# Attention of two batches in step, its second tiles in the weights' empty half, and x of the last two batches through device memory

## The chip, the cores and the metric

The kernel runs on one core of one Trainium2 chip. The time is device microseconds of one execution, given as the median of several runs. TensorE (PE) multiplies, with weight loads shown apart as PEld; VectorE (DVE), ScalarE (ACT) and GpSimd (POOL) work on tiles; SyncE (SP) issues most of the DMA transfers.

## The reference

Everything is float32 except the two weight matrices, which arrive as float64. Shapes: four batches, eight heads, 768 positions, head size 64; the heads side by side give rows of 512.

```python
# decaying attention, block of 64 positions, lam per head
intra = (qb @ kb.T * Dmask) @ vb              # Dmask[i,j] = lam**(i-j) for i >= j
inter = (qb * lam**(pos+1)) @ kv_state
out[block] = intra + inter
kv_state = lam**64 * kv_state + (kb * lam**(63-pos)).T @ vb
...
x = out, heads side by side                    # (4, 768, 512)
u = x + real(fft(fft(x, axis=1), axis=2))
un = (u - mean(u)) / sqrt(var(u) + 1e-6)       # per row of 512
return u + max(un @ w_ch1, 0) @ w_ch2          # 512 x 2048, 2048 x 512
```

## The kernel before

**Attention** goes in chunks of 128 positions (two reference blocks in one), six a batch. `attn(b)` is a generator that writes the instructions of one batch, chunk by chunk. `attn_in` loads k, q and v (256 KB each), multiplies k by its decays on POOL, turns K and Q on TensorE (L314, L319) and copies them back through ScalarE (L316, L321); VectorE makes the decayed queries qs. `attn_out` makes the scores (L338), which VectorE multiplies by the decays into sc (L343), updates the state (L358 on TensorE, then POOL and VectorE), and adds the product of queries and state (L373) to that of scores and v (L379). The result oT is turned back into rows of x (L395). Batch 0 is kept turned as well (`TURNED`), and batch 1 follows it without a break, its first loads under batch 0's last chunk (`LEADS`). These two use states of 64 rows. Batches 2 and 3 use a "padded" state of 128 rows, sd, that ScalarE fills. Their attention is woven chunk by chunk into the products of the MLP.

**The transform and the layer norm** are `fft_ln(b)`. Rows and mirrored rows are folded on VectorE (L476 to L571); the mirrored ones are gathered by POOL's DMA from a copy of x in device memory. Then come products with tables of cosines and sines (L603), the transform over the width (L615 to L620), sums and the normalised rows un (L634 to L691), and transposes of these to ut (L660).

**The weights** arrive as float64 and are decoded in 32 pieces of 512 KB (`load_weights`): a load into a tile raw, Sign and Relu on ScalarE (L225, L228), and five steps on VectorE (L226, L230, L232, L234, L235). The tile raw comes from the same pool of four buffers as hr, the MLP's hidden rows. The tile e is scratch of the decoding. Both matrices stay in SBUF for the whole kernel. The first half of w1's columns and of w2's rows is decoded first, then the second half.

**The MLP** runs plainly for four groups of half a batch each (`PLAIN`): first product L749 into a PSUM bank pm, ReLU into hr on ScalarE (L757) or VectorE (L755), second product L763. The first three of these are done in two halves of the hidden width, so that the first halves can go ahead of the second half of the weights. The other four groups wait and go through a scheme that saves products by sums of blocks: `combine_weights` (L837) and `front_sums` make sums of the weights (w1s and others), and L1031, L1198 and L1124 are its products. This late stage begins at 409.57 us. Its rows are ur, its sums of rows sx.

**What sets the order.** All these generators are woven into one text by `beside` and `weave`, which draw from two generators in proportion to estimated times. A scheduler then sets each engine's row; a few instructions are held in the order written (`keep_in_program_order`). Each engine works through its row in order. PSUM is shared by two pools of banks: pa (`psum_a`) for attention and transform, pm (`psum_m`) for the MLP.

```python
run(beside(att0, NC * t_chunk - 2.7, w, 0.25 * NW))
...
fr = chain([att1, fft_ln(1)] + [front(b) for b in range(2, B)])
...
back = chain(half[1] + [mlp(*PLAIN[3])])
run(weave(fr, back, (t_back - t_half) / (t_rest - t_rest * t_half / t_back)))
```

Of the kernel before, what the change touches and what calls it, by code (L numbers as in the profile page):

```python
# [77 lines left out]
def kernel(  # L78
# [207 lines left out]
    def attn(b):  # L286

        head = () if b - 1 in LEADS else attn_in(b, 0)
        for c in range(NC):
            yield from head  # L290
            head = attn_in(b, c + 1) if c < NC - 1 else attn_in(b + 1, 0) if b in LEADS else ()
            yield from attn_out(b, c, head)

    ins, oTs, eo = {}, {}, {}
    LEADS = (0,)
# [3 lines left out]
    def attn_in(b, c):  # L299
        rows = slice(c * C, (c + 1) * C)  # L300
        kt, qt, vt = (new(ld, [C, H, D], nm) for nm in ("k", "q", "v"))
        for t, src in ((kt, k), (qt, q), (vt, v)):
            nc.sync.dma_start(t, src[b, :, rows, :].rearrange("h p d -> p h d"))
        if b == 0:
            load_tables(c)

        kd = None
        if c < NC - 1:
            kd = new(at, [C, H, D], "kd")
            nc.gpsimd.tensor_tensor(kd, kt, kpow, op=ALU.mult)  # L310

        ptk = psum_a([128, HP, C])
        for hp in range(HP):
            nc.tensor.transpose(ptk[:, hp, :], pair(kt, hp), ident)  # L314
        kT = new(at, [128, HP, C], "kT")
        nc.scalar.copy(kT, ptk)  # L316
        ptq = psum_a([128, HP, C])
        for hp in range(HP):
            nc.tensor.transpose(ptq[:, hp, :], pair(qt, hp), ident)  # L319
        qT = new(at, [128, HP, C], "qT")  # L320
        nc.scalar.copy(qT, ptq)  # L321
        qs = None
        if c > 0:
            qs = new(at, [128, HP, C], "qs")
            nc.vector.tensor_tensor(qs, ptq, qpow, op=ALU.mult)
        ins[b, c] = kT, qT, qs, kd, vt
        yield 1.2

    def attn_out(b, c, head):
        kT, qT, qs, kd, vt = ins.pop((b, c))  # L330
        last = c == NC - 1
        padded = b not in TURNED and b - 1 not in LEADS

        mm = nc.tensor.matmul
        pss = [psum_a([C, HP, C]) for _ in range(2)]
        for hp in range(HP):
            for hi in range(2):
                mm(pss[hi][:, hp, :], lhsT=kT[HD[hi], hp, :], rhs=qT[HD[hi], hp, :], start=True, stop=True)  # L338
        sc = []
        for hi in range(2):  # L340
            t = new(at, [C, HP, C], "sc", bufs=3)
            with tc.high_priority(100) if not padded else ExitStack():
                nc.vector.tensor_tensor(t, pss[hi], decay[:, hi::2, :], op=ALU.mult)  # L343
            sc.append(t)
        if last and b - 1 in LEADS:
            mirror_a(b, pin=True)
        yield 2.4 if padded and not last else 1.5


        s_old, s_new = (st, st) if padded else (turns_of[(c + 1) % 2], turns_of[c % 2])  # L350
        if padded and c == 0:
            nc.gpsimd.memset(sd, 0.0)
        if not last:
            pu = psum_a([128, HP, D])
            for hp in range(HP):
                for hi in range(2):
                    h = 2 * hp + hi
                    mm(pu[HD[hi], hp, :], lhsT=kd[:, h, :], rhs=vt[:, h, :], start=True, stop=True)  # L358
            if c == 0:
                nc.vector.tensor_copy(s_new, pu)  # L360
            else:
                nc.gpsimd.tensor_tensor(s_new, s_old, spow.broadcast_to([128, HP, D]), op=ALU.mult)
                grown = nc.vector.tensor_tensor(s_new, s_new, pu, op=ALU.add)
            if not padded:
                yield 0.9


        po = psum_a([128, HP, C])
        if c > 0:
            for hp in range(HP):  # L370
                for hi in range(2):
                    old, qh = (sd[:, hp, hi, :], qs[:, hp, :]) if padded else (s_old[HD[hi], hp, :], qs[HD[hi], hp, :])
                    mm(po[HD[hi], hp, :], lhsT=old, rhs=qh, start=(hp == 0), stop=False, skip_group_check=True)  # L373
        if padded and not last:
            for hi in range(2):
                nc.scalar.copy(sd[HD[hi], :, hi, :], st[HD[hi]])
        for hp in range(HP):
            for hi in (1, 0) if padded else (0, 1):
                mm(po[HD[hi], hp, :], lhsT=vt[:, 2 * hp + hi, :], rhs=sc[hi][:, hp, :],  # L379
                   start=(c == 0 and hp == 0), stop=(hp == HP - 1), skip_group_check=True)  # L380
        oT = new(at, [128, HP, C], "oT")
        nc.scalar.copy(oT, po)
        if b in TURNED:

            if c == 0:
                nc.scalar.copy(first, po[:, :, 0:1])
            elif c > 1:
                nc.scalar.copy(oTs[b][:, :, 0:1], po[:, :, 0:1])
        yield 2.0
        yield from head  # L390

        def turn(oT):
            px = psum_a([C, HP, 128])
            for hp in range(HP):
                nc.tensor.transpose(px[:, hp, :], oT[:, hp, :], ident)  # L395
            return px.rearrange("p h e -> p (h e)")

        def put(px, x, n=128):
            nc.scalar.copy(x[0:n, 0:HM], px[0:n, 0:HM])
            nc.scalar.copy(x[0:n, HM:DM], px[0:n, DM - 1:HM - 1:-1])  # L400

        def back(oT, x):
            put(turn(oT), x)

        if b not in TURNED:
            x = xn_[b, c] = new(xp, [C, DM], "x") if c < HC else new(xn, [C, DM], "xn")
            back(oT, x)
            if c == 0:
                xd[b] = (dram.tile([S - 256, DM], F32, name=f"xa{b}"), dram.tile([257, DM], F32, name=f"xb{b}"))
                nc.scalar.dma_start(xd[b][1][256:257], x[0:1])  # L410
            elif not last:
# [10 lines left out]
            yield 1.7  # L422
            return

# [11 lines left out]
        px = turn(oTs[b]) if c > 1 else None  # L436
# [6 lines left out]
        if c > 1:  # L443
            mirrored(c - 1, px)
            yield 1.4
        if not last:
            x = xn_[b, c] = new(xp, [C, DM], "x") if c < HC else new(xn, [C, DM], "xn")
            back(oT, x)
            yield 1.7
        else:  # L450
            mirrored(c, turn(oTs[b]))
            for t in range(HC):
                xs[b, t] = xn_.pop((b, t))
            yield 1.4
# [4 lines left out]

    uts, utd, ud, held = {}, {}, {}, {}  # L460
# [22 lines left out]
    def mirror_a(b, pin=False):  # L483

        xa = xd[b][0]

        eo[b] = new_eo()
        for a, n in enumerate(BLK):
            i = gather(out=eo[b][a][1][0:n, 1, 0:DM], out_offset=None, in_=xa[:, :], in_offset=row_of(a, n))
            if pin:  # L490

                tc.keep_in_program_order(i)
        for t in range(2, HC):
            u = xs[b, HC + t] = new(xp, [128, DM], "x")
            i = gather(out=u[:, :], out_offset=None, in_=xa[:, :], in_offset=row_of(2 + t))
            if pin:
                tc.keep_in_program_order(i)

    def mirror_b(b):
        for t in range(2):  # L500
            u = xs[b, HC + t] = new(xp, [128, DM], "x")
            gather(out=u[:, :], out_offset=None, in_=xd[b][1][:, :], in_offset=row_of(2 + t))
# [75 lines left out]
    def fft_ln(b):  # L578
# [11 lines left out]
        else:  # L590
            yield 1.0
# [744 lines left out]
    def front(b):  # L1336
        yield from attn(b)
        yield from fft_ln(b)

# [29 lines left out]
    t_chunk = 7.3  # L1369
    t_front = NC * t_chunk + 13.0 + 7.0 + 5.7 + 3 * 2.4  # L1370
# [4 lines left out]

    att1, mix = attn(1), fft_ln(0)
    att0 = attn(0)
    run(part(att0, 2.7))
# [59 lines left out]
```

## Time and profile before

| | |
|---|---|
| time, median of 3 runs | 775.78 us (774.68 to 776.88) |
| profiled execution, span | 771.7 us, 15006 instructions; no other time is given for it |
| PE busy | 752.6 us (98%) |
| PEld busy | 646.7 us (84%) |
| DVE busy | 602.8 us (78%) |
| ACT busy | 231.1 us (30%) |
| POOL busy | 178.4 us (23%) |
| DMA | 120.22 MB, mean 156 GB/s |

The span runs from the first to the last instruction of the execution. A line of the timeline gives start in us, duration in us, engine, source line, operation, output<-inputs, shapes, and in brackets how long the engine had stood idle ahead of it and what ended that. A line of the chain gives start, duration, engine, output tile, source line and number of instructions. A line of the windows gives the window, its length, then busy time and number of instructions of PE, PEld, DVE, ACT and POOL, the granted TensorE clock, the mean share of busy DMA engines and GB/s. A group's line ends with its busy time, the mean ns of one, and the idle time ahead of it. A DMA line gives KB each and the median us from issue to landing.

### The profile page before, as it was taken

To read this page: it belongs to the slowest core of one execution; us is meant where nothing else is said; L and a number is where in the kernel's file an instruction comes from. 1 tells how busy PE (TensorE), PEld (TensorE's weight loads), DVE (VectorE), ACT (ScalarE), POOL (GpSimd) and SP (SyncE) were. 2 spreads that over 40 slices of the span, in tenths; PEclk is the share of its full clock that TensorE was granted. 3 is DMA by queue.
4 is the path that set the end of the run, shared out by engine and by line. 5 is a ranking of instruction groups with operands and counts; after the bars stand their busy time and mean duration, and the time that the engine had idled before them with its cause. 6 is when DMAs were issued, how large, how long until landed. Compare 5 with 4: busy or idle time off the path is not lost.

```text
span 771.7 us, 15006 instructions
## 1 busy us (share of the span) xinstructions
PE 752.6 (98%) x5784; PEld 646.7 (84%) x5784; DVE 602.8 (78%) x1167; ACT 231.1 (30%) x532; POOL 178.4 (23%) x202
## 2 busy tenths in 40 slices
PE   6989999999999999999999999999999999999997
PEld 5777877777685967769747899999999999999997
DVE  6999998784936575336898999788986699758984
ACT  3755443435521221322101221034301341024310
POOL 3223330021111113220105941360015001230013
PEclk9999999999999999999999999999999999999999
DMA  9979732347943149731433465876545456455442
GB/s 240 274 161 250 195 125 86 106 96 181 246 117 94 45 82 270 176 97 35 113 65 124 150 218 164 273 234 202 180 124 178 125 186 182 127 175 180 144 141 70
DMA packets 154924, 120.22 MB, mean 156 GB/s; under 512 B 114286, under 2 KB 116974, under 8 KB 154854
## 3 DMA queue, kind: packets, MB, share of 16 engines
q1 hardware_dynamic: 147792, 100.51, 46.7%
q0 software_dynamic: 4032, 12.99, 4.7%
q10 hardware_dynamic: 3030, 5.78, 2.1%
q8 instruction: 46, 0.75, 0.4%
q14 instruction: 24, 0.20, 0.1%
HBM read 88.04 MB, written 31.20 MB: 155 GB/s over the span
## 4 chain that ended last, share of the span: by engine, by line
PE 88%; DVE 7%; DMA 2%; ACT 1%; issue 1%; POOL 0%; SPq 0%; DVEq 0%; ACTq 0%
PE p L1198 22%; PE p L1124 17%; PE pm L763 13%; PE pm L749 13%; PE p L1031 6%; PE pa L603 3%; PE pa L379 3%; PE pa L338 3%; PE pa L373 2%; PE pa L314 1%; PE pa L358 1%; PE pa L395 1%; DVE sc L343 1%; PE pa L763 1%; PE pa L319 1%
## 5 line engine op out<-in xcount | busy, mean ns | idle before, releaser
L749 PE MATMUL pm<-ut,w 128*128 128x256 f32 x512 | 118.3, 381 | 0.0
L763 PE MATMUL pm<-w,hr 128*128 128x512 f32 x240 | 108.7, 596 | 0.1
L749 PEld LDWEIGHTS pm<-ut,w 128*128 128x128 f32 x512 | 94.7, 190 | 14.4 <-issue 2.7
L763 PEld LDWEIGHTS pm<-w,hr 128*128 128x128 f32 x240 | 43.8, 190 | 45.5 <-issue 43.8
L1219 POOL TENSOR_TENSOR y<-y,u 128x512 f32<-128x512 f32 x12 | 19.9, 1661 | 186.8 <-DVE y L1228 155.5
L1198 PE MATMUL p<-tx,sx 128*128 128x128 f32 x400 | 52.7, 275 | 0.0
L1198 PEld LDWEIGHTS p<-tx,sx 128*128 128x128 f32 x400 | 48.6, 192 | 0.0
L1133 DVE TENSOR_TENSOR ha<-p,ha 128x512 f32<-128x512 f32 x60 | 40.1, 686 | 8.6 <-PE p L1124 8.6
L1204 ACT COPY y<-p 128x128 f32<-128x128 f32 x48 | 12.8, 266 | 103.6 <-PE p L1198 103.1
L310 POOL TENSOR_TENSOR kd<-k,decay 128x512 f32<-128x512 f32 x20 | 21.7, 1083 | 86.5 <-PE pa L358 50.1
L343 DVE TENSOR_TENSOR sc<-pa,decay 128x512 f32<-128x512 f32 x48 | 30.9, 683 | 11.7 <-PE pa L338 11.5
L1206 DVE TENSOR_TENSOR y<-p,y 128x128 f32<-128x128 f32 x92 | 25.6, 285 | 15.6 <-PE p L1198 9.1
L1198 PE MATMUL p<-w,ha 128*128 128x128 f32 x288 | 37.4, 275 | 0.0
L1133 DVE TENSOR_TENSOR hs<-p,hs 128x512 f32<-128x512 f32 x39 | 26.2, 685 | 12.4 <-PE p L1124 12.4
L338 PEld LDWEIGHTS pa<-qT,kT 64*128 64x128 f32 x384 | 25.1, 193 | 12.2 <-ACT qT L321 6.4
L1198 PEld LDWEIGHTS p<-w,ha 128*128 128x128 f32 x288 | 34.9, 192 | 0.1
L638 POOL TENSOR_SCALAR ve<-mv 128x2 f32<-128x2 f32 x12 | 6.2, 519 | 120.0 <-DVE mv L635 120.0
L757 ACT ACTIVATE hr<-pm 128x256 f32<-128x256 f32 x44 | 16.7, 382 | 57.6 <-PE pm L749 53.7
L1124 PE MATMUL p<-sx,tx 128*128 128x128 f32 x264 | 33.9, 275 | 0.0
L338 PE MATMUL pa<-qT,kT 64*128 64x128 f32 x384 | 30.1, 292 | 2.9 <-ACT qT L321 2.9
L1124 PEld LDWEIGHTS p<-sx,tx 128*128 128x128 f32 x264 | 31.7, 192 | 0.0
L379 PE MATMUL pa<-sc,v 128*64 128x128 f32 x384 | 28.9, 282 | 1.3 <-DVE sc L343 1.0
(274 smaller groups left out, 1748.4 us busy)
## 6 DMA issues: line engine op xcount, KB each, us to landing
tx<-td SPq DMA_DIRECT2D x84, 256.0 KB, 2.9
raw<-in_moe_w_ch_dram SPq DMA_DIRECT2D x32, 512.0 KB, 4.3
tx<-sd SPq DMA_DIRECT2D x63, 256.0 KB, 2.8
k<-in_k_dram SPq DMA_DIRECT2D x24, 256.0 KB, 3.7
q<-in_q_dram SPq DMA_DIRECT2D x24, 256.0 KB, 7.0
v<-in_v_dram SPq DMA_DIRECT2D x24, 256.0 KB, 5.7
td<-tx SPq DMA_DIRECT2D x21, 256.0 KB, 2.0
ud<-x SPq DMA_DIRECT2D x16, 256.0 KB, 3.1
```

What stands on the lines that cost most here:

```text
L310: nc.gpsimd.tensor_tensor(kd, kt, kpow, op=ALU.mult)
L338: mm(pss[hi][:, hp, :], lhsT=kT[HD[hi], hp, :], rhs=qT[HD[hi], hp, :], start=True, stop=True)
L343: nc.vector.tensor_tensor(t, pss[hi], decay[:, hi::2, :], op=ALU.mult)
L379: mm(po[HD[hi], hp, :], lhsT=vt[:, 2 * hp + hi, :], rhs=sc[hi][:, hp, :], start=(c == 0 and hp == 0), stop=(hp == HP - 1), skip_group_chec ...
L603: mm = nc.tensor.matmul(ps[:, n, :], lhsT=piece(a, i, n), rhs=cs[0:rows, a, i in (2, 3), n, :], start=(a == 0), stop=(a == 1))
L749: nc.tensor.matmul(ps, lhsT=w1[:, c, 128 * fc:128 * fc + 128], rhs=ut[:, c, :], start=(c == 0), stop=(c == KO - 1))
L763: return nc.tensor.matmul(ps, lhsT=hr[(fc - f0) // 4][:, fc % 4, 128 * i:128 * i + 128], rhs=w2[:, fc, :], start=(fc == f0), stop=(fc == f ...
L1031: nc.tensor.matmul(ps, lhsT=s2.A[a][:, kt, 128 * i:128 * i + 128], rhs=U[b][:, kt, :], start=(first and kt == 0), stop=(kt == 1), skip_gro ...
L1124: nc.tensor.matmul(ps[:, 128 * i:128 * i + 128], lhsT=ab[m][0][:, 128 * i:128 * i + 128], rhs=ab[m][1], start=(start and i == 0), stop=Tru ...
L1133: V.tensor_tensor(o, p, o, op=ADD)
L1198: nc.tensor.matmul(ps[:, 0:HM // 2], lhsT=ab[m][0][i], rhs=ab[m][1][:, i, :], start=(start and i == 0), stop=(i == HF // 2 - 1), skip_grou ...
L1206: V.tensor_tensor(o, ps[:, 0:HM // 2], o, op=ADD)
```

## The change

**Attention by steps.** `attention()` takes the place of `attn(b)`. A step is one chunk of two batches, first (0, 1), then (2, 3): turnings of K of both, of Q of both, scores of both, products with the state of both, state updates of both, and so on. All batches use states of 64 rows; the padded ones are gone. The next step's loads are issued at the start of a step.

**Where the second batch's tiles lie.** Batches 1 and 3 use no tiles of the pools: theirs are `spare`, slices of the second half of w2 and of w1, before these halves are decoded. (In the rows of the orders below, w_129 is w1 and w_130 is w2: where they stand in a line of attention, they are k, q, oT or another tile of the second batch.) PSUM tiles of attention alternate between pa and pm for as long as `early` is set.

**x of batches 2 and 3.** It is stored to device memory in all its rows (a third buffer, xc, for chunk 0) and loaded again in `mirrors(b)`, which also holds all gathers and is called at the start of `fft_ln(b)`.

**The order.** All attention is written ahead of the rest: the first batches' steps beside a quarter of the weights, the next ones beside the transform of batch 0 and 0.125, and the last step beside the first 12 us of the MLP and another 0.125. Then `fft_ln(1)`, `fft_ln(2)`, `front_sums` and `fft_ln(3)` stand beside the remaining half of the weights and the MLP. The late stage is as before.

```diff
-    st = const.tile([128, HP, D], F32, name="st")
-    sd = const.tile([128, HP, 2, D], F32, name="sd")
-    turns_of = [st, sd[:, 0:HP // 2].rearrange("p h a d -> p (h a) d")]
+    turns_a = [const.tile([128, HP, D], F32, name=n) for n in ("st", "sd")]
...
+    TWOS = ((0, 1), (2, 3))
+    spare = [w2[:, FO // 2 + i, :] for i in range(FO // 2)]
+    spare += [w1[:, c, DFF // 2 + DM * i:DFF // 2 + DM * (i + 1)] for c in range(KO) for i in range(2)]
...
+    def psum_t(shape):
+        bank_of[0] += 1
+        if early[0] and bank_of[0] % 8 in (1, 4, 6):
+            return psum_m(shape)
+        return psum_a(shape)
...
+        def tile(self, shape, name, i=None):
+            if self.two:
+                t = place[name if i is None else f"{name}{i % 2}"]
+                return t.rearrange("p (h d) -> p h d", h=shape[1])
+            return new(ld if name in "kqv" else at, shape, name, **({"bufs": 2} if name == "sc" else {}))
...
-            if (b, c) == (B - 1, 1):
-                with tc.issue_after(grown.ins):
-                    run(front_sums())
-            if c == NC - 2 and b - 1 not in LEADS:
-                mirror_a(b)
-            elif last:
-                mirror_b(b)
...
+    def attention():
+        steps = [([sides[b] for b in two], c) for two in TWOS for c in range(NC)]
...
+            for s in then:
+                s.load(c_)
...
+            for s in two:
+                scores(s, c)
+            yield 2.2
+            for s in two:
+                from_state(s, c)
+            if c < NC - 1:
+                for s in two:
+                    to_state(s, c)
+            yield 2.8
+            for s in two:
+                within(s, c)
+            yield 2.0
+            for f in (turn_k, turn_q):
+                for s in then:
+                    f(s, c_)
+                yield 0.6
+            for s in two:
+                back(s, c)
+                yield 0.9
...
+    def mirrors(b):
+        xa, xb, xc = xd[b]
+        eo[b] = new_eo()
...
+        if (b, 0) not in xn_:
+            for c in range(HC + 2):
+                x = xn_[b, c] = new(xp, [C, DM], "x") if c < HC else new(xn, [C, DM], "xn")
+                nc.sync.dma_start(x, xc if c == 0 else xa[(c - 1) * C:c * C])
...
-    run(beside(att0, NC * t_chunk - 2.7, w, 0.25 * NW))
-    run(beside(part(mix, T_FOLD), T_FOLD, att1, 3.25 * t_chunk))
-    run(beside(mix, 24.0, beside(att1, 2.75 * t_chunk, w, 0.16 * NW), 0.16 * NW + 1.75 * t_chunk))
+    run(beside(part(att, NC * t_step), NC * t_step, w, 0.25 * NW))
+    run(beside(part(mix, T_FOLD), T_FOLD, att, 2.0 * t_step))
+    run(beside(mix, 24.0, beside(att, 2.0 * t_step, w, 0.125 * NW), 0.125 * NW + 2.0 * t_step))
+    early[0] = False
...
-    fr = chain([att1, fft_ln(1)] + [front(b) for b in range(2, B)])
+    fr = chain([fft_ln(1), fft_ln(2), front_sums(), fft_ln(3)])
...
-    run(beside(beside(chain(half[0]), t_half, w, 0.5 * NW), t_half + 0.5 * NW, fr, t_rest * t_half / t_back + 15.0))
+    lead = chain(half[0])
+    run(beside(part(lead, 12.0), 12.0, beside(w, 0.125 * NW, att, t_step), 0.125 * NW + t_step))
+    run(att)
+    run(beside(lead, t_half - 12.0, beside(w, 0.5 * NW, fr, t_rest * t_half / t_back), 0.5 * NW + t_rest * t_half / t_back))
```

TensorE's row within attention, before, in a chunk of batch 0: one batch's transposes, then its scores and the state.

```order
L314 MATMUL pa_310<-ident,k_301 128x128 x4
L319 MATMUL pa_317<-ident,q_302 128x128 x4
L395 MATMUL pa_332<-ident,oT_299 128x128 x4
L338 MATMUL pa_339<-qT_322,kT_315 128x128
L338 MATMUL pa_340<-qT_322,kT_315 128x128
```

And after, in a step of batches 0 and 1 (L340 turns K, L348 Q, L403 turns back, L373 is the product with the state, L380 the state's update):

```order
L340 MATMUL pa_434<-ident,k_334 128x128 x4
L340 MATMUL pm_442<-ident,w_130 128x128 x4
L348 MATMUL pa_448<-ident,q_335 128x128 x4
L348 MATMUL pm_457<-ident,w_130 128x128 x4
L403 MATMUL pa_467<-ident,oT_418 128x128 x4
L403 MATMUL pa_482<-ident,w_129 128x128 x4
...
L373 MATMUL pa_525<-qs_455,sd 64x128 x8
L373 MATMUL pm_534<-w_129,w_130 64x128 x8
L380 MATMUL pa_543<-v_336,kd_432 64x64 x8
L380 MATMUL pa_554<-w_130 64x64 x8
```

Each kind of product now stands twice in a row, once for each batch, in different banks.

ScalarE's row at the MLP's first group, before: the ReLUs (L757) alternate with the Sign and Relu steps of single weight pieces.

```order
L757 ACTIVATE hr_1383<-pm_1419 128x256
L757 ACTIVATE hr_1383<-pm_1425 128x256
L225 ACTIVATE e_1432<-raw_1431 128x512
L228 ACTIVATE e_1432<-e_1432,cvt 128x512
L757 ACTIVATE hr_1472<-pm_1467 128x256
```

And after (L223 is the Sign, L226 the Relu of the decoding, L791 the ReLU of the MLP):

```order
L223 ACTIVATE e_2305<-raw_2304 128x512
L226 ACTIVATE e_2305<-e_2305,cvt 128x512
L223 ACTIVATE e_2315<-raw_2314 128x512
L791 ACTIVATE hr_2367<-pm_2362 128x256
L791 ACTIVATE hr_2367<-pm_2378 128x256
L226 ACTIVATE e_2315<-e_2315,cvt 128x512
L223 ACTIVATE e_2325<-raw_2324 128x512
```

The fifth ReLU of the first group (onto hr_2367) now stands behind the Sign of the last piece but one; the pieces ahead of it stand without MLP steps between them. On VectorE the same pieces end so, with the layer norm's un (L689) and the MLP's sums (L827) behind them:

```order
L224 TENSOR_SCALAR e_2325<-raw_2324 128x512
...
L233 SCALAR_TENSOR_TENSOR w_130<-w_130,e_2325 128x512
L689 TENSOR_SCALAR un_2426<-x_1120,mv_2116,rs_2124 128x256 x2
L827 TENSOR_TENSOR x_466<-pm_2406,x_466 128x256
```

TensorE's row ahead of the late stage, before: the last second products of the MLP stand right ahead of the first late ones.

```order
L763 MATMUL pm_3808<-w_130,hr_3566 128x512 x4
L763 MATMUL pm_3808<-w_130,hr_3678 128x512 x4
L1031 MATMUL p_3864<-ur_3775,w_129 128x256 x2
...
L1031 MATMUL p_3864<-sx_3858,w1s 128x256 x2
```

And after (L650 to L654 are the transform over the width of batch 3, L1065 is the late stage's first product):

```order
L651 MATMUL pa_3627<-dt,ys_136 128x129
L652 MATMUL pa_3627<-dt,ys_133 128x128
L1065 MATMUL p_3751<-ur_3704,w_129 128x256 x2
...
L1065 MATMUL p_3751<-sx_3745,w1s 128x256 x2
```

The MLP's products are no longer there: they stand ahead of the transform of batch 3.

More of the change, by code (lines that the diff above doesn't have):

```diff
@@ L340, in attn_out @@
         for hi in range(2):
-            t = new(at, [C, HP, C], "sc", bufs=3)
-            with tc.high_priority(100) if not padded else ExitStack():
+            t = s.tile([C, HP, C], "sc", hi)
+            with tc.high_priority(100):
                 nc.vector.tensor_tensor(t, pss[hi], decay[:, hi::2, :], op=ALU.mult)
[L344 to L365, printed above, removed]
@@ L368, in attn_out @@
-        po = psum_a([128, HP, C])
-        if c > 0:
[L370 to L380, printed above, removed]
@@ L385, in attn_out, with within @@
+    def within(s, c):
+        n, po = s.now, s.now["po"]
+        lead(mm(po[HD[hi], hp, :], lhsT=n["vt"][:, 2 * hp + hi, :], rhs=n["sc"][hi][:, hp, :],
+                start=(c == 0 and hp == 0), stop=(hp == HP - 1), skip_group_check=True)
+             for hp in range(HP) for hi in range(2))
+        n["oT"] = s.tile([128, HP, C], "oT")
+        nc.scalar.copy(n["oT"], po)
+        if s.b in TURNED:
             if c == 0:
@@ L590, in fft_ln @@
         else:
-            yield 1.0
+            mirrors(b)
+            yield 6.0
             run(fold_a(b))
```

199 lines of the change are left out of this document (107 added, 92 removed).

## Prediction

> **What bounds the kernel now.** I read the busy line and the chain of the page first, then the windows, then TensorE's groups, then the timelines of the places that the change moves.
>
> ```profile
> PE 752.6 (98%) x5784; PEld 646.7 (84%) x5784; DVE 602.8 (78%) x1167; ACT 231.1 (30%) x532; POOL 178.4 (23%) x202
> PE 88%; DVE 7%; DMA 2%; ACT 1%; issue 1%; POOL 0%; SPq 0%; DVEq 0%; ACTq 0%
> ```
> ```profile
> 0.00:20.00 20.00, 13.69 (x135) 10.85 (x136) 13.56 (x29) 7.28 (x14) 6.78 (x19) 1.00 1.01 242
> 20.00:40.00 20.00, 18.82 (x243) 15.85 (x242) 19.44 (x36) 15.51 (x36) 5.05 (x5) 1.00 1.11 273
> 100.00:120.00 20.00, 20.00 (x79) 14.05 (x78) 19.08 (x50) 7.82 (x19) 6.20 (x4) 1.00 0.27 92
> 380.00:400.00 20.00, 19.85 (x51) 9.38 (x50) 19.18 (x33) 0.38 (x1) 0.93 (x2) 1.00 0.44 114
> ```
> TensorE holds the chain, but VectorE (DVE, the third busy column) is at 19 of 20 us while the weights are decoded (20 to 40, 100 to 120) and while they are combined (380 to 400). There it is hidden only as long as TensorE has independent work queued. So I count TensorE's work and look for what it waits for.
>
> ```profile
> L749 PE MATMUL pm<-ut,w 128*128 128x256 f32 x512 | 118.3, 381 | 0.0
> L763 PE MATMUL pm<-w,hr 128*128 128x512 f32 x240 | 108.7, 596 | 0.1
> L763 PE MATMUL pa<-w,hr 128*128 128x512 f32 x16 | 7.4, 592 | 0.0
> L603 PE MATMUL pa<-cs,fe 128*128 128x193 f32 (+1 forms) x96 | 17.2, 327 | 0.0
> L603 PE MATMUL pa<-cs,fo 128*128 128x193 f32 (+1 forms) x64 | 11.6, 328 | 0.0
> L616 PE MATMUL pa<-dt,ys 128*128 128x129 f32 x32 | 6.2, 275 | 0.0
> ...
> L660 PE MATMUL pa<-ident,un 128*128 128x128 f32 x24 | 3.6, 273 | 0.0
> ```
> ```profile
> 98.83 5.18 PE pm L749 x24
> ...
> 165.00 1.09 PE pa L338 x16
> 166.09 1.06 PE pm L749 x4
> ...
> 354.00 2.63 PE pa L603 x16
> ...
> 382.00 27.73 PE pm L763 x64
> ```
> In these chain rows matmuls run back to back (a record is one of the two passes of an f32 product): 0.216 us for an L749 record, 0.43 for L763, 0.164 for L603. That gives 512 x 0.216 + 256 x 0.43 + 160 x 0.164 = 247 us. One dense attention chunk:
>
> ```profile
> 54.51 1.16 PE L338 MATMUL pa<-qT,kT 64*128 64x128 f32 x16
> 55.60 0.69 PE L358 MATMUL pa<-v,kd 128*64 128x64 f32 x16
> 56.21 1.09 PE L373 MATMUL pa<-qs,st 64*64 64x128 f32 x16
> 57.23 1.29 PE L379 MATMUL pa<-sc,v 128*64 128x128 f32 x16
> 58.46 0.66 PE L314 MATMUL pa<-ident,k 128*128 128x128 f32 x4
> ...
> 59.39 0.60 PE L395 MATMUL pa<-ident,oT 128*128 128x128 f32 x4
> ```
> From 54.51 to about 59.8 (four L395 last 0.44 to 0.49, 0.11 each) is 5.3 us a chunk. Chunks 0 lack L373 and chunks 5 lack L358, so 24 chunks are about 122. Widths and the transposes of the layer norm, 176 records from L615 to L660 at about 0.11, add 19. All together 388 us, and the late stage (L1031) starts at 409.6, so TensorE is idle for some 21 us before it: 5 for the first load, the rest almost all in the first 95 us.
>
> **Part 1, chunks in pairs: worth 7 us.** A group that uses half of the array's rows or columns pays at its ends: the four L749 records behind L338 (166.09) take 1.06 instead of 0.86, so 0.2 a change. A chunk changes three times, 0.6 us. With both batches' groups side by side a step of two chunks pays 0.6 once: 2 x 5.3 - 0.6 = 10.0. Twelve steps save 7.2 us (between 0 and 8). The padded L373 is replaced by the 64-row form at the same spacing: nothing. The ScalarE copies of padded states vanish on an idle engine: nothing.
>
> **Part 2, waits inside attention.** Before, the first 12 chunks waited 15 us besides the first load. After, the first scores need six loads instead of three, so I put the start at 8 (5 to 10). Inside a step the other batch covers: 0.5 a step, 6 us (0 to 25, the upper end if transfers set the pace, below). Attention then ends near 136: 12 x 10.0, less the missing groups, plus 7.7 of the first transform, plus 14.
>
> **Part 3, the decode behind attention: 36 us of wait.** Twelve weight pieces are decoded before attention ends. The other 20 stand in VectorE's row as one block behind it. ScalarE's row has the fifth ReLU of the first MLP group (onto hr_2367) behind the Sign of piece 19, and hr shares its buffers with the raw pieces. TensorE may run three pm banks ahead, so it stops at the eighth product of that group. One piece costs:
>
> ```profile
> 123.12 0.42 DVE L226 TENSOR_SCALAR e<-raw 128x512 uint16<-128x512 uint16 x1
> ...
> 125.44 0.69 DVE L235 SCALAR_TENSOR_TENSOR w<-w,e 128x512 f32<-128x512 f32 x1
> ...
> 130.00 0.43 DVE L226 TENSOR_SCALAR e<-raw 128x512 uint16<-128x512 uint16 x1 [2.13 <-DMA raw<-in_moe_w_ch_dram]
> ```
> ```profile
> raw<-in_moe_w_ch_dram SPq DMA_DIRECT2D x32, 512.0 KB, 4.3
> ```
> From 123.12 to 125.44 one each of L226, L235, L230, L234 and L232 start: 2.32 us. Three raw buffers (the fourth holds hr_2132), each 4.3 for the load, 2.4 to be read and 0.3 to be issued, allow one per 2.33. So 2.3 a piece (2.2 to 2.9, as the 2.13 wait shows). The block starts 13.5 us after attention (19 rows of layer norm, and two normalisations that wait for transposes), and 17.6 pieces must pass: 13.5 + 40.5 + 1.3 for Sign and ReLU = 55. TensorE has 18.5 us of work by then: the second batch's last group, widths, transposes and seven products of 1.73. The wait is 36 us (28 to 52). The normalisation un_2426 at the block's end is due at 61, TensorE's transposes of it at 69: not the binding one.
>
> **Part 4, the tail without cover: 40 us of wait.** Before, the last MLP group's 27.7 us (382.00 above) ran over the layer norm of batch 3 and the combining of weights. After, the same products stand ahead of that transform. VectorE's chain, by the present one:
>
> ```profile
> 344.35 0.68 DVE L476 TENSOR_TENSOR fe<-fo,xn 128x512 f32<-128x512 f32 x1
> 358.96 0.42 DVE L542 TENSOR_TENSOR fo<-fo 65x256 f32<-65x256 f32 x1
> 367.43 0.42 DVE L691 TENSOR_TENSOR ds<-pa,bs 128x256 f32<-128x256 f32 x1 [5.58 <-ACT ds L687]
> 386.69 2.36 DVE L837 TENSOR_TENSOR w1s<-w 128x1024 f32<-128x1024 f32 x2 [0.82 <-POOL rs L639]
> 404.09 4.59 DVE L837 TENSOR_TENSOR w<-w 128x1024 f32<-128x1024 f32 x4
> 411.26 0.68 DVE L929 TENSOR_TENSOR sx<-ur 128x512 f32<-128x512 f32 x1
> 411.98 0.69 DVE L931 TENSOR_TENSOR sx<-ur,sx 128x512 f32<-128x512 f32 x1
> ```
> ```profile
> 409.57 5.61 PE L1031 MATMUL p<-ur,w 128*128 128x256 f32 x24
> 415.02 1.03 PE L1031 MATMUL p<-sx,w1s 128*128 128x256 f32 x4
> ```
> ```profile
> sd<-fe POOLq DMA_DIRECT2D x5, 256.0 KB, 4.6
> ```
> Folds 15.0; then 5 until L691 (it was 8 with MLP products between); layer norm 18 (19.3 here, 14 without its waits); combining 22.0; the two sums 1.4: 61 us until the first product that reads w1s. The folds start 8.5 us after the last-but-one row block of L763, since the partial sums of the weights now use the same fe buffer and its store takes 4.6. TensorE has 13.7 of L763, 6.6 of L603, 4.0 of widths and 5.4 of L1031 meanwhile: 29.7. The wait is 8.5 + 61 - 29.7 = 40 us (28 to 50). From there the order is as before: 415.02 to the end.
>
> **Part 5, x through device memory.** Ten more loads and two more stores of 256 KB. They are issued long before the folds; nothing, unless transfers bound attention. POOL's gathers move to one place and wait there: nothing.
>
> **Part 6, restarting after a long wait.** The first groups are slow:
>
> ```profile
> 5.05 1.08 PE L314 MATMUL pa<-ident,k 128*128 128x128 f32 x4 [5.05 <-DMA k<-in_k_dram]
> 7.96 2.08 PE L338 MATMUL pa<-qT,kT 64*128 64x128 f32 x16 [0.68 <-ACT qT L321]
> ```
> 1.08 against 0.66 for four L314, 2.08 against 1.16 for sixteen L338, and the granted clock of that window still reads 1.00. The excess until it is gone is about 2 us, so I take 2 for each of the two long waits, 4 in all (0 to 6). Without this term the forecast would be 4 less. The Trainium skill, TensorE: Matmul & The Clock Gate (Part 1, the HAM clock gate), says that the array falls to half its clock after an idle window of about 3.4 us and needs about 3.4 us of work to come back. By that rule the two restarts cost an estimated 3.4 us, and the forecast would be 841. The slow first rows agree with it.
>
> **Sum.** 388 - 7 of work, 14 of start and attention waits, 36, 40 and 4: 475 us until what is 409.6 now, so 66 us more (475.4 without rounding). The profiled span 771.7 becomes about 837.5. The runs' median, 775.8, lies 4.1 above that span, so 842.
>
> **Rivals.** *Only one of the two waits appears.* For it: VectorE might have decoded ahead, or the combining might start earlier. Against it: each engine runs its row in order, and both blocks are behind what TensorE must deliver. Leaving out 36 and a restart gives 804, leaving out 40 gives 800. *Transfers set the pace of attention.* The windows show the DMA share at 1.01 and 1.11 with 242 and 273 GB/s when one batch ran. A step needs six 256 KB loads, a raw piece or so and up to 0.8 MB of stores, some 2.2 to 2.5 MB, 9 to 10 us at 250 GB/s. At 12 us a step the end is 20 later: 862. *Faster.* If TensorE were never without work behind attention, only the pairs' 7 us and 7 of shorter waits would show: 762. It decides only if 17.6 pieces pass in the 5 us that TensorE has left after the block's start, 0.3 us a piece against 2.3; VectorE at 19.08 of 20 at 100 to 120 speaks against it. *No effect* would need gain and waits to cancel at 14 us of wait.
>
> **Chances.** Both waits 0.70 (own range 824 to 860), transfers on top 0.10, one wait alone 0.14: slower 0.94. Faster 0.04. Within 0.3% (what a measurement of this kernel can tell from no change) 0.02. To hold 8 in 10 the range is 812 to 866: it takes the lower ends of both waits and the slow transfers, and leaves out one-wait cases and faster.
>
> **What would show it.** Attention over by 130 to 145. Right behind it TensorE near empty for about 36 us while VectorE is full with L224 to L233, TensorE resuming after an ACTIVATE on hr. A second hole of about 40 us before L1065 with VectorE full of folds and L871. Slow first groups after each. The part after it as long as before, 357 us. I am wrong if TensorE's windows stay near 20 behind attention, if the pieces run at over 3.5 or under 1.5 us, or if attention itself ends after 150.

## The result and the profile after

The changed kernel takes 858.07 us (856.82 to 859.28, 4 runs) against 775.62 before: 1.105 times as long, 95% interval 1.103 to 1.108. Its profiled span is 857.4 us. The first fence has the busy line and the chain by engine, the second the windows behind attention and ahead of the late stage.

```profile
PE 759.0 (89%) x5784; PEld 659.5 (77%) x5784; DVE 604.4 (70%) x1167; ACT 224.9 (26%) x512; POOL 170.6 (20%) x200
PE 73%; DVE 15%; DMA 7%; issue 2%; ACT 1%; SPq 1%; POOL 1%; DVEq 0%; ACTq 0%; POOLq 0%
```
```profile
80.00:100.00 20.00, 17.12 (x226) 15.68 (x224) 19.97 (x36) 7.84 (x17) 7.36 (x8) 0.91 0.97 205
100.00:120.00 20.00, 16.97 (x158) 15.33 (x156) 15.03 (x30) 8.79 (x19) 4.04 (x4) 0.83 0.63 160
160.00:180.00 20.00, 7.49 (x37) 6.26 (x35) 17.86 (x44) 10.75 (x18) 0.93 (x2) 0.77 0.66 214
180.00:200.00 20.00, 0.00 (x0) 0.00 (x0) 19.74 (x45) 11.75 (x19) 0.00 (x0) 0.50 0.69 220
...
460.00:480.00 20.00, 4.75 (x11) 3.87 (x12) 17.20 (x39) 0.97 (x4) 2.79 (x6) 0.61 0.50 125
480.00:500.00 20.00, 5.44 (x18) 4.25 (x17) 19.31 (x24) 0.74 (x2) 0.00 (x0) 0.67 0.36 80
```

The work is the same (5784 matmuls; VectorE 604 us against 603), but TensorE's share fell from 98 to 89%. Two holes stand out, 167 to 206 and 440 to 498; in the windows shown of both, VectorE is busy for 17 to 20 of 20 us. The granted clock reads 0.50 in the window without a single matmul. TensorE's timeline at the two places:

```profile
163.87 3.62 PE L783 MATMUL pm<-ut,w 128*128 128x256 f32 x16
205.69 3.78 PE L783 MATMUL pm<-ut,w 128*128 128x256 f32 x8 [38.20 <-ACT hr L791]
209.26 1.06 PE L694 MATMUL pa<-ident,un 128*128 128x128 f32 x4
210.11 6.98 PE L797 MATMUL pm<-w,hr 128*128 128x512 f32 x14
216.93 1.89 PE L783 MATMUL pm<-ut,w 128*128 128x256 f32 x8
...
416.20 24.20 PE L797 MATMUL pm<-w,hr 128*128 128x512 f32 x56
443.46 0.63 PE L637 MATMUL pa<-cs,fe 128*128 128x193 f32 x2 [3.07 <-DVE fe L559]
444.47 7.42 PE L637 MATMUL pa<-cs,fe 128*128 128x193 f32 x22 [0.37 <-DVE fe L564]
...
475.25 8.45 PE L1065 MATMUL p<-ur,w 128*128 128x256 f32 x24 [15.58 <-DVE w1s L871]
498.25 2.04 PE L1065 MATMUL p<-sx,w1s 128*128 128x256 f32 x4 [14.56 <-DVE sx L965]
```

TensorE stops in the MLP's first group and goes on when ScalarE's ReLU onto hr comes, 38.20 us later. From 440.4, the end of the last MLP product, to 498.25, where the late stage gets its first sums, 57.9 us pass in which it has 16 us of work at full speed. The first groups after a hole are slow: eight L783 records take 3.78 instead of 1.89. Attention's last group starts at 149.72.

### The profile page after: what moved, and what is told of

The parts are those of the page before. It is cut to its first block, busy times and chain, and to the rows that moved or that the text cites. A ratio compares the mean times of both kernels' runs of the same rounds, so it can differ in the third digit from the quotient of the medians.

```text
span 857.4 us, 14963 instructions
## 1 busy us (share of the span) xinstructions
PE 759.0 (89%) x5784; PEld 659.5 (77%) x5784; DVE 604.4 (70%) x1167; ACT 224.9 (26%) x512; POOL 170.6 (20%) x200
## 4 chain that ended last, share of the span: by engine, by line
PE 73%; DVE 15%; DMA 7%; issue 2%; ACT 1%; SPq 1%; POOL 1%; DVEq 0%; ACTq 0%; POOLq 0%
PE p L1232 19%; PE p L1158 15%; PE pm L783 12%; PE pm L797 11%; PE pa L637 4%; PE p L1065 4%; DMA raw<-in_moe_w_ch_dram 3%; DMA w<-in_k_dram 2%; DVE w L230 1%; PE pa L360 1%; PE pa L797 1%; DVE w L233 1%; DMA w<-in_q_dram 1%; PE pa L373 1%; DVE e L232 1%
## 5 line engine op out<-in xcount | busy, mean ns | idle before, releaser
L783 PE MATMUL pm<-ut,w 128*128 128x256 f32 x512 | 115.7, 383 | 38.2 <-ACT hr L791 38.2
L783 PEld LDWEIGHTS pm<-ut,w 128*128 128x128 f32 x512 | 97.5, 192 | 54.5 <-ACT hr L791 38.6
L797 PE MATMUL pm<-w,hr 128*128 128x512 f32 x240 | 105.6, 596 | 0.0
L797 PEld LDWEIGHTS pm<-w,hr 128*128 128x128 f32 x240 | 45.7, 192 | 53.0 <-issue 52.4
L1253 POOL TENSOR_TENSOR y<-y,u 128x512 f32<-128x512 f32 x12 | 19.9, 1661 | 186.8 <-DVE y L1262 100.4
L791 ACT ACTIVATE hr<-pm 128x256 f32<-128x256 f32 x44 | 16.7, 382 | 133.2 <-PE pm L783 132.7
L772 POOL DMA_INDIRECT out_dram<-y,ix x12 | 13.4, 1120 | 182.8 <-DVE y L832 171.0
L827 DVE TENSOR_TENSOR x<-pm,x 128x256 f32<-128x256 f32 x5 | 2.1, 425 | 65.4 <-PE pm L797 65.4
L1065 PE MATMUL p<-ur,w 128*128 128x256 f32 x96 | 27.0, 428 | 15.6 <-DVE w1s L871 15.6
L1065 PEld LDWEIGHTS p<-ur,w 128*128 128x128 f32 x96 | 20.9, 219 | 19.3 <-issue 15.7
L789 DVE TENSOR_SCALAR hr<-pm 128x256 f32<-128x256 f32 x20 | 8.4, 419 | 31.9 <-PE pm L783 31.9
L1065 PE MATMUL p<-sx,w1s 128*128 128x256 f32 x64 | 17.2, 398 | 14.6 <-DVE sx L965 14.6
```

The source lines that it names most:

```text
L772: nc.gpsimd.indirect_dma_start(out=out_high, out_offset=row_of(2 + HC * (b + 1) + T - HC), in_=y[:, :], in_offset=None)
L783: nc.tensor.matmul(ps, lhsT=w1[:, c, 128 * fc:128 * fc + 128], rhs=ut[:, c, :], start=(c == 0), stop=(c == KO - 1))
L791: nc.scalar.activation(t, ps, AF.Relu)
L797: return nc.tensor.matmul(ps, lhsT=hr[(fc - f0) // 4][:, fc % 4, 128 * i:128 * i + 128], rhs=w2[:, fc, :], start=(fc == f0), stop=(fc == f ...
L1065: nc.tensor.matmul(ps, lhsT=s2.A[a][:, kt, 128 * i:128 * i + 128], rhs=U[b][:, kt, :], start=(first and kt == 0), stop=(kt == 1), skip_gro ...
L1253: nc.gpsimd.tensor_tensor(o, y, u, op=ADD)
```

## The experiments

Unless a section says otherwise, times are medians of 4 executions, and the kernel before, measured beside them, took 774.3 to 774.6.

**Why 20 pieces stood in one block.** The text of the change has the cause. `weave` ends, when its second generator has nothing left, by writing all that is left of the first at once:

```python
if d is None:
    return t_lead + sum(lead)
```

By then attention was used up: the weave beside `mix` had run it out in the same way. So `beside(w, 0.125 * NW, att, t_step)` wrote all 20 remaining pieces on the spot. The same line had a second effect. With no weights left, the next weave wrote the whole first half of the MLP without `fr` beside it. The transforms thus began behind the whole first half of the MLP (`t_half`, planned at 81.6 us) instead of behind its first 12 us, and the MLP ran out ahead of batch 3's transform. So the order that the section on the change describes, with attention's last step beside the MLP's first 12 us and the transforms beside the rest of the weights, was never written. The first two experiments mend one effect each.

**front_only**

```diff
-    run(beside(part(lead, 12.0), 12.0, beside(w, 0.125 * NW, att, t_step), 0.125 * NW + t_step))
+    run(beside(part(lead, 12.0), 12.0, w, 0.125 * NW))
...
-    run(beside(lead, t_half - 12.0, beside(w, 0.5 * NW, fr, t_rest * t_half / t_back), 0.5 * NW + t_rest * t_half / t_back))
+    run(beside(lead, t_half - 12.0, w, 0.5 * NW))
```

> The last 20 weight pieces are written one by one beside the first halves of the MLP instead of all at once behind attention; nothing else is moved. Theory (the hole of 38.2 us is the block of pieces, written as one): the hole goes, its slow restart of 3 us with it, and the tail's hole stays: 858 - 41 = 817 us (810 to 825). Rival (the pieces' 46 us of VectorE must pass before the MLP's second halves in any case, so the wait only moves behind the first halves): 840 us or more, with a hole of over 20 us further back.

Measured: 814.74 us, 43 less. The theory holds. All 20 pieces still come behind attention, and behind it TensorE no longer waits for any of them; the tail's waits stay, as the two largest lines of TensorE's waits show (us in all, times, longest):

```profile
PE p L1065 <- DVE sx L965: 15.4, 1, 15.4
PE p L1065 <- DMA ur<-utd: 15.2, 1, 15.2
```

**tail_only**

```diff
-    run(weave(fr, back, (t_back - t_half) / (t_rest - t_rest * t_half / t_back)))
+    run(weave(fr, back, (t_half + t_mlp - 54.0) / 136.7))
```

> The MLP's products are drawn more slowly beside the transforms, so that the last group's second products stand between the transform of batch 3 and the late stage, as before the change; the block of pieces stays. Theory (the tail's 42 us are lost cover): 27.7 us of products lie over the layer norm and the combining again, and the folds start earlier: 858 - 38 = 820 us (812 to 830), and no PE gap over 5 us between 430 and the late stage. Rival (VectorE's chain from the folds on is the bound, whatever TensorE has beside it): the products only run inside the hole of the same end, 850 us or more.

Measured: 839.48 us, 19 less: half of what the theory said, more than the rival. The products now stand between the transform and the late stage, but other waits have come in. TensorE's timeline of this kernel and the lines of its waits:

```profile
409.90 2.54 PE L783 MATMUL pm<-ut,w 128*128 128x256 f32 x8 [3.68 <-DVE hr L789]
...
440.20 11.43 PE L797 MATMUL pm<-w,hr 128*128 128x512 f32 x26 [3.21 <-DVE hr L789]
457.46 19.02 PE L797 MATMUL pm<-w,hr 128*128 128x512 f32 x38 [5.83 <-DVE hr L789]
```
```profile
PE pm L797 <- DVE hr L789: 13.3, 3, 5.8
PE pm L783 <- DVE hr L789: 3.7, 1, 3.7
```

In the second halves of the MLP every other ReLU runs on VectorE (L789). There it stands behind folds, layer norm and combining, so 17 us of the gain were lost again to waits for it (13.3 and 3.7).

**both**: the two edits together.

> Both edits together. Theory (two separate holes): the gains add, 858 - 41 - 38 = 779 us (770 to 790), so about as before the change, since attention itself takes 14 us more than I had forecast and the pairs save 7. Rival (one VectorE backlog behind both holes): the gains don't add; 800 us or more.

Measured: 800.29 us, 57.8 less than the change. The time is at the rival's bound of 800, but its reason does not hold: the two gains, as each was measured alone, add but for 4 us (43.3 + 18.6 = 61.9). What is missing against the 779 forecast was missing in tail_only already: 15.1 us of waits for L789 are left (11.6 and 3.5 in two lines of its waits).

**both_act**

```diff
-            if fc % 2 and f1 == FO:
+            if False:
```

> Both edits as before, and all ReLUs of the MLP's second halves on ScalarE; in the former they alternate with VectorE, where TensorE waited 15.1 us for them behind folds, layer norm and combining. Theory (the tail's missing gain was turned into waits for these ReLUs): the waits go, and with them a slow restart: 800 - 17 = 783 us (778 to 788). Rival (VectorE's combining is the bound of the tail whatever the ReLUs do): the wait moves to L1065, 797 us or more.

Measured: 787.75 us, 12.5 less. The waits for L789 are gone. A new line heads TensorE's waits:

```profile
PE p L1065 <- DVE y L832: 13.2, 1, 13.2
```

Part of the rival is true too: the late products now wait for the MLP's last sums, which stand in VectorE's row behind the combining. So in the tail the wait went from one VectorE instruction to the next and shrank each time: 33.6 us in the changed kernel, 17 in tail_only, 13 here.

**before_no_cover**: the kernel before, with its cover taken away.

```diff
-    run(weave(fr, back, (t_back - t_half) / (t_rest - t_rest * t_half / t_back)))
+    run(weave(fr, back, 1.7 * (t_back - t_half) / (t_rest - t_rest * t_half / t_back)))
```

> The kernel before, with the plain MLP groups drawn 1.7 times as fast beside attention and transforms, so that the last group's products stand ahead of the transform of batch 3, as in the changed kernel; nothing else. Theory (the tail's loss is the missing cover alone): 775 + 38 = 813 us (800 to 825), with gaps ahead of the late stage behind VectorE's combining. Rival (the loss comes from the changed attention or x through device memory): within 8 us of 775.

Measured: 824.34 us, 50 more than before, just inside the expected range's upper end of 825. Its timeline has the tail's hole without any of the change's attention or transfers (L603 is the transform, L1031 the late stage):

```profile
410.22 8.42 PE L603 MATMUL pa<-cs,fe 128*128 128x193 f32 x24 [8.17 <-DVE fe L526]
...
435.58 8.31 PE L1031 MATMUL p<-ur,w 128*128 128x256 f32 x24 [9.10 <-DMA ur<-utd]
465.10 2.05 PE L1031 MATMUL p<-sx,w1s 128*128 128x256 f32 x4 [21.20 <-DVE sx L931]
```

The first sums of the late stage come 50 us later than before (465.10 against 415.02), which is the whole loss. So drawing the MLP's products too early makes such a hole by itself.

**short_decode**: L230 and L232 left out for the last 20 pieces.

```diff
+        if landed[0] <= 12:
             nc.vector.scalar_tensor_tensor(dst, lo, 2.0 ** -32, d, op0=ALU.mult, op1=ALU.add)
             nc.vector.tensor_tensor(p, p, sg, op=ALU.mult)
```

> The changed kernel, with two of the five VectorE steps (low word and sign product, 0.94 us of 2.3) left out for the last 20 pieces, so that its weights are not the right ones. If VectorE sets the pace of the block, 17.6 pieces x 0.94 = 16 us less: 842 us. If the load through three buffers sets it (4.6 us of load, 0.3 of issue and the reads, over three), the pace falls only from 2.3 to about 1.9: 7 us less, 851 us.

Measured: 846.11 us, 12 less, between the two. The hole shrank from 38.2 to 28.9 us; the other 3.4 us of the gain came ahead of it, since attention's last group started at 146.30 instead of 149.72, though the edit leaves the first 12 pieces and attention as they were. The chain through the hole now goes from load to load, three pieces every 5.4 to 6.3 us:

```profile
167.67 3.91 DMA raw<-in_moe_w_ch_dram
...
173.11 4.15 DMA raw<-in_moe_w_ch_dram
...
178.78 4.76 DMA raw<-in_moe_w_ch_dram
...
185.07 4.25 DMA raw<-in_moe_w_ch_dram
```

So a piece costs some 1.9 us by the load through three buffers, and VectorE's 2.3 was just above it. With the block written as it is, making VectorE alone or the loads alone faster would not have closed the hole.

**half_loads**: the changed kernel, odd chunks on the tiles of the even ones.

```diff
+                if c_ % 2:
+                    s.kqv[c_] = s.kqv_last
+                else:
                     s.load(c_)
+                s.kqv_last = s.kqv[c_]
```

> The changed kernel, where every odd chunk computes on the tiles of the even chunk ahead of it, so half of the loads of q, k and v are left out. If transfers cost attention all of the 14 us by which it ended later than forecast: 858 - 14 = 844 us, attention over at 136. If they cost the waits that the trace puts on K and Q, 7 us without the first load, and VectorE the rest: 850 us, with the waits on qs and the folds between 80 and 110 still there. If the loads are hidden: 858.

Measured: 859.17 us, no gain, although the DMA share of 40 to 80 (next to last column) fell from about 1.0 in the changed kernel, the first two lines, to 0.6 here, the last two:

```profile
40.00:60.00 20.00, 19.70 (x304) 17.80 (x305) 14.46 (x26) 12.47 (x30) 4.48 (x6) 1.00 0.99 243
60.00:80.00 20.00, 17.32 (x241) 15.33 (x238) 12.31 (x25) 13.74 (x34) 3.21 (x3) 1.00 1.02 251
...
40.00:60.00 20.00, 15.65 (x186) 14.21 (x181) 12.46 (x21) 10.46 (x25) 6.04 (x7) 0.83 0.61 144
60.00:80.00 20.00, 18.49 (x264) 16.02 (x263) 17.75 (x32) 11.94 (x29) 2.63 (x2) 1.00 0.59 160
```

Loads still came late, but because they were issued late. Up to 160 us SyncE's queue stood 23.2 us at loads of weight pieces (L212) whose buffers VectorE had not yet read, and V of the second batch, queued behind them, was issued at 45.10: TensorE waited 3.7 us for it. The edit itself holds the queue too. A tile that serves two chunks is free later, so the loads of attention (L323) stood 45.1 us until the products with V (L390) had read it, against 15.9 in the changed kernel. First the queue's lines, then TensorE's:

```profile
SPq L323 <- PE pm L390: 24.1, 3, 17.9
SPq L212 <- DVE w L230: 23.2, 5, 8.8
SPq L323 <- PE pa L390: 21.0, 3, 10.9
```
```profile
PE pa L380 <- DMA w<-in_v_dram: 3.7, 1, 3.7
```

Half the loads gave no gain, but with these longer holds the run alone does not clear the transfers. The next one says more.

**att_alone**: both_act with nothing beside attention (one execution, 805.04 us in all).

```diff
-    run(beside(part(att, NC * t_step), NC * t_step, w, 0.25 * NW))
-    run(beside(part(mix, T_FOLD), T_FOLD, att, 2.0 * t_step))
-    run(beside(mix, 24.0, beside(att, 2.0 * t_step, w, 0.125 * NW), 0.125 * NW + 2.0 * t_step))
+    run(att)
+    run(beside(mix, 40.0, w, 0.375 * NW))
```

> The kernel with spread weights, restored tail and ScalarE's ReLUs, with nothing written beside attention: all 12 steps first, then the transform of batch 0 and the weights. The total will be worse; what is read is the end of attention (149 to 151 in the changed kernel, with 8 us of transform in it; forecast 136). Theory (VectorE's folds and decoding ahead of qs and sc, and SyncE's row that stands behind raw loads, cost the 14 us): attention ends at 8.5 + 117 = 126, at most 130. Rival (its own loads of 1.5 MB a step set the pace): steps stay at 11 to 12 us, end at 138 or later.

Its attention's last group starts at 121.72, so it ends at 122.4. TensorE is full from 20 to 60, at the same DMA share of 1.0 that the changed kernel had, with VectorE at half (windows; then the last group):

```profile
20.00:40.00 20.00, 20.00 (x324) 18.73 (x322) 9.74 (x17) 10.30 (x27) 6.47 (x8) 1.00 1.01 224
40.00:60.00 20.00, 20.00 (x320) 18.74 (x318) 9.23 (x16) 11.07 (x30) 5.35 (x6) 1.00 0.98 219
```
```profile
121.72 0.65 PE L403 MATMUL pa<-ident,w 128*128 128x128 f32 x4
```

So attention's own loads do not hold it at a share of 1.0. With the raw loads beside them a share near 1.0 need not hold it either: in the changed kernel TensorE was busy for 19.70 of 20 us from 40 to 60, at 0.99 (the first line under half_loads). In the changed kernel attention ended at 150.4, with 7.7 us of the first transform's products and 1.1 of widths in it. The other 19 us are due to what is written beside it: folds and decoding on VectorE, and the raw loads in SyncE's queue. How much is due to each wasn't separated. In both_act, which has the same text for attention, it ended at 146.5, so some 4 of the 19 us differ between kernels for a reason that no run shows. The trace tells in what form the time went: TensorE was idle for 20.3 us instead of 9.35, and the 1712 records of attention kept it busy for some 119 us instead of 113.05.

**by_need, best2, best3, best4**: steps towards a kernel that keeps the pairs without the holes, each on top of the one ahead. by_need issues the six loads of a step as K, K, Q, Q, V, V:

```diff
-            for s in then:
-                s.load(c_)
+            load_by_need(then, c_)
```

> The kernel with ScalarE's ReLUs, and the six loads of a step issued by need: K of both batches, Q of both, V of both, instead of K, Q, V of one batch and then of the other. Theory (attention loses to transfers that land in the wrong order): waits on K and Q of the second batch, 5.5 us, go, the start is 1 to 2 us earlier, and the half clock behind them goes too: 7 us less than the former, 776 us. Rival (the bandwidth itself sets the pace): V is late instead, within 2 us of the former.

Measured: 784.40 us (780.73 to 788.77) against 787.75, some 3 less, with overlapping runs: inconclusive. In its trace the 5.0 us of waits for the second batch's K are gone, but the waits for qs have grown from 4.3 to 6.3 us.

best2 (6 executions):

```diff
+            with tc.high_priority(100):
                 nc.vector.tensor_tensor(n["qs"], pt, qpow, op=ALU.mult)
...
+                with tc.high_priority(200):
                     tt(y[:, 0:HM], ps[:, 0:HM], u[:, 0:HM], op=ALU.add)
                     tt(y[:, HM:DM], ps[:, HM:DM], u[:, DM - 1:HM - 1:-1], op=ALU.add)
...
-    run(weave(fr, back, (t_half + t_mlp - 54.0) / 136.7))
+    run(weave(fr, back, (t_half + t_mlp - 64.0) / 136.7))
```

> The kernel with loads by need, with qs taken ahead of other work on VectorE, the sums of the MLP's last rows taken ahead of the combining, and the MLP drawn a little more slowly. If VectorE's order is what is left (4.4 us of wait on qs, 9.5 us on the sums): 784 - 10 = 774 us, about the time before. If the combining itself is the bound: the wait moves to L1065's sums and 2 to 4 us are gained, 781 us.

Measured: 785.60 us, no gain. The wait on qs fell to 0.4 us, but 5.2 us on a fold of the first transform came in its place, and the wait on the last sums, 9.5 us in by_need, was 11.0.

best3 (12 executions): the output rows y of the MLP get two buffers.

```diff
-                y = new(up, [128, DM], "y", bufs=1)
+                y = new(up, [128, DM], "y", bufs=2)
```

> The same with two buffers for the output rows of the MLP, since the last sum waited 3.1 us for a store. If that store was on the path: 2 to 3 us less than with one buffer. If not: the same within 1 us.

Measured: 779.33 us, 6 less, twice what was expected. The wait on the last sums fell from 11.0 to 2.2 us, here in best2 and then in best3:

```profile
PE p L1074 <- DVE y L841: 11.0, 1, 11.0
...
PE p L1074 <- DVE y L841: 2.2, 1, 2.2
```

With one buffer the sums stood behind all of the combining in VectorE's row and then waited 3.0 us for the store of the row ahead, until 420.95. With two they stand ahead of its last three steps, start at 413.42 and wait for no store.

best4 (12 executions):

```diff
-    run(beside(part(mix, T_FOLD), T_FOLD, att, 2.0 * t_step))
-    run(beside(mix, 24.0, beside(att, 2.0 * t_step, w, 0.125 * NW), 0.125 * NW + 2.0 * t_step))
+    run(beside(part(mix, T_FOLD), T_FOLD, att, 3.0 * t_step))
+    run(beside(mix, 24.0, att, 3.0 * t_step))
...
-    run(beside(part(lead, 12.0), 12.0, w, 0.125 * NW))
+    run(beside(part(lead, 12.0), 12.0, w, 0.25 * NW))
```

> The kernel with two buffers for output rows (779 us), with four weight pieces moved from the transform of batch 0 to the MLP's first group, and the folds of batch 0 spread over three steps of attention instead of two. If VectorE's backlog at 80 to 110 costs attention its time (a wait of 5.2 us on a fold, half a clock window behind it): the waits between 80 and 120 shrink by 4 to 7 us, 774 us (771 to 777). If the folds' number alone counts: unchanged, 779 us. If the MLP's first group has to wait for the moved pieces: 785 us or more.

Measured: 772.70 us against 775.18 for the kernel before, measured beside it: 0.997 times as long, 95% interval 0.996 to 0.999. One of the 12 executions took 2585.79 us; the other eleven lie between 771.93 and 776.29, and the interval is theirs. The median is 6.6 us under that of best3, as forecast, and the wait on the fold is gone. Its busy line and its windows of attention:

```profile
PE 743.7 (96%) x5784; PEld 645.9 (84%) x5784; DVE 598.5 (78%) x1147; ACT 231.7 (30%) x532; POOL 175.6 (23%) x200
```
```profile
80.00:100.00 20.00, 17.05 (x241) 15.36 (x240) 19.96 (x39) 8.36 (x21) 8.04 (x6) 1.00 1.10 245
100.00:120.00 20.00, 18.99 (x258) 17.32 (x256) 11.72 (x23) 7.95 (x17) 6.93 (x8) 1.00 0.73 164
```

The window 100 to 120 holds 2 us more of TensorE than in the changed kernel and is at full clock. TensorE's busy time is now 743.7 us instead of 752.6. The pairs are in this gain, but so is that attention no longer stands between the MLP's products; no run separates the two.

## Why the prediction was right, and where a step was off

The forecast was 842 us (812 to 866); measured 858. Against the forecast span of 837.5, the 857.4 has 19.9 us more. 14 of them are attention's end, 2 the first wait, and 4 the slow restarts and the late stage's slow start.

- **Part 1, pairs worth 7 us.** Borne out in the main. In att_alone the records of attention keep TensorE busy for 113.05 us; the forecast had 114 for them (136 less 14 and 7.7). TensorE's busy time in best4 is 8.9 us under that of before, both near full clock, though not all of it need be the pairs'. In the changed kernel itself the gain was hidden, since stretches at a lower clock brought busy time to 759.0.
- **Part 2, waits inside attention.** This term was mis-sized: 14 us of start and waits, with attention over at 136. It ended at 150.4, past the 150 that the prediction named as a sign of being wrong. TensorE was idle for 20.3 us instead of 14, and busy for 130.1 where the forecast had 122. The starting point was misread as well. The 21 us of idle time before were what the sum of products left over, 409.6 less 388; in the trace TensorE is busy for 396.7 of the 409.6 us, so 12.9 were idle, and the rest were products slower than the back-to-back pace. The waits in the first 95 us were thus some 7 us besides the first load, not 15. The upper end of the waits inside a step was 25, but for transfers that set the pace. att_alone speaks against that reason and shows another: what VectorE and SyncE's queue were given beside attention. The prediction had VectorE at 19 of 20 us in three windows of before, and used it only for what stands behind attention.
- **Part 3, 36 us of wait.** 38.2 measured, ended by the very ReLU that was named. TensorE's stop came 17.1 us after attention (18.5 forecast), its restart 55.3 after (55 forecast). The Signs of the block's pieces came 2.35 us apart (18 steps from 161.78 to 204.14; 2.3 forecast). short_decode shows the load's 1.9 us just under it. front_only shows that the block as written was the cause: 20 pieces spread out cost nothing, so the space lent to attention was not the price.
- **Part 4, 40 us of wait.** Four gaps of 33.6 us in all, and 8 lost to slow records: 57.9 - 16 = 41.9, against 40 and a restart of 2. The sum is right and the split is not: VectorE's chain sets the end of this stretch (62.7 us from the first fold at 435.39 to the sums, 61 forecast), so what slow products took came out of the wait. before_no_cover shows the mechanism alone. What the step did not see is that VectorE's own ReLUs and sums would hold the cover itself (tail_only, both_act).
- **Part 5, x through memory: nothing.** Borne out as far as TensorE's waits go: none names those loads. But one of them (L532) held SyncE's queue for 17.1 us, with the block's first raw loads behind it, the first issued at 155.27, and ScalarE's first Sign of the block then waited 2.7 us for a load. It wasn't tried alone, so a cost of nothing is not shown.
- **Part 6, restarts of 2 us each.** Behind the first hole the three slow groups (3.78, 1.06, 6.98) cost some 3.1 us more than at full speed (1.89, 0.60 and about 6.2). The Trainium skill, TensorE: Matmul & The Clock Gate (Part 1, the HAM clock gate), has the array at half its clock after an idle window. The trace agrees: 0.50 granted at 180 to 200, and 3.78 against 1.89 right behind it. The 3.4 us that the prediction estimated by that rule for two restarts are too few: the first alone cost 3.1.
- **The rivals.** One wait alone did not occur; "faster" would have needed 0.3 us a piece. The rival of slow transfers gave 862, close to the result and for the wrong reason. The range's upper end of 866 stood for it, so that the range had room for attention's late end is in part luck.

## What to carry to other kernels

Read where each block of work of a full side engine stands in its row, and ask what the main engine has queued for that time: here some 600 us of VectorE work cost nothing or 80 us by its place. When cover is put back, look at what the cover itself needs from the full engine (its ReLUs, its sums, an output buffer), since the wait moves there. And a scheme that weaves by estimates should keep weaving when one side runs out; a remainder written at once is a block.

## What was not expected of the hardware

A DMA share near 1.0 did not by itself slow attention. In att_alone, with no weight pieces in SyncE's queue and no folds or decoding on VectorE, TensorE was busy 20.00 of 20 us at shares of 0.98 to 1.01. In half_loads, at a share of 0.61, it was at 15.65 in the window in which it waited 3.7 us for a load that had stood in the issuing queue. And one buffer more for a row of 256 KB was worth 6 us, though the wait for its store was 3.0 us, because the sums also moved ahead of the last steps of the combining.
